# The third mixer burst of a batch moves from behind tile 0 to behind the 64-row tile 24

## The chip, the cores and the metric

One core of a Trainium2 chip runs the kernel. The metric is device time in microseconds (us), taken as the median of several runs. The engines are TensorE (PE, its weight loads PEld), VectorE (DVE), ScalarE (ACT), GpSimd (POOL) and SyncE (SP). Transfers are issued from SP (all DMA transposes, and the stores of the last batch) and from POOL (all loads, and the other stores).

## What is computed

Eight batches, each with a gated attention without softmax and, on its result, a low-rank token mixer and a channel mixer:

```python
scores = (1/S) * z @ z.T                  # S = 3136, z has 64 columns
x      = u * (max(scores, 0)**2 @ v)      # u, v, x: 3136 x 256
xm     = x + (x.T @ U @ V).T              # rank 32
out    = xm + max(xm @ w_ch1, 0) @ w_ch2  # 256 -> 1024 -> 256
```

## The kernel before

**Tiles.** The 3136 rows of a batch are 25 row tiles: 24 of 128 rows, and tile 24 (`NF`) of 64. Output tiles are worked off in the order 12, 13, ..., 24, 0, 1, ..., 11 (`turns(i) = (12 + i) % 25`), so place `i` = 12 is tile 24 and place 13 is tile 0. `FIRST` is 12 and `AHEAD` is 4.

**Scores and strips.** The squared scores are symmetric, so `A[j]` holds only 13 blocks, (j, j) to (j, j+12). `score_steps(b, j, k0, k1)` gives the steps that make blocks k0 to k1: two matmuls into one of two buffers of a PSUM pair (L307), a relu on ACT (L320), a square on DVE (L322). The other 12 blocks that output tile o needs are transposes: `turn(b, o)` issues one DMA transpose on SP (L342) of `A[o][:, 128:]` into a `strip`, one of five buffers that go round in the order of the calls. `attend_steps(b, o)` gives the 25 steps of an output tile; steps 0 to 12 read blocks of `A`, the later ones the strip of o. In steady work `turn` is called four places ahead, at the end of place `i` for the tile of place `i + 4`. Batch 0 starts before all scores are there, so it has its own tables: `first_at` says which scores are made within which place (spread evenly over its 25 steps), `first_turns` which strips are turned at the end of it:

```python
if b == 0 and i in first_turns:
    for t in first_turns[i]:
        turn(b, t)
elif i + AHEAD < NT:
    turn(b, turns(i + AHEAD))
```

**Accumulators.** An output tile accumulates in two PSUM banks, one for the upper and one for the lower 64 rows of every block (L380, matmuls that use 64 rows and 128 columns of the array, two of them side by side). Two tiles share a set of two banks: (0, 1), (2, 3), ..., (22, 23); tile 24 has a set alone. Tile 24 uses quarters of the array, 64 by 64 (L420). There are two sets, taken in turn: `open_pair` takes `sets[opened[0] % 2]` and counts `opened` up; `spare()` gives the set that no open pair holds, or, when none is open, the one that was opened last. `close_pair` adds the two banks (ACT L394, DVE L395) and multiplies by u into `x_bf` (DVE L410); for tile 24 two more copies on ACT (L406) and an addition on DVE (L407) stand between, in batch 0 four additions (L403).

**The mixer.** In places of batch b the mixer of batch b-1 runs, in 7 chunks of up to four tiles. `low_rank(b, c)` adds the low-rank part (L546, L560) and turns the chunk for the next product with a DMA transpose on SP (`turn_x`, L519, tile `ut`); chunks 4 and 5 have it within places 10 and 11. A burst n is the up-projection of chunk n (L578, full 128 by 128 array, relu on ACT L596, through the two PSUM pair buffers) merged with the down-projection of chunk n-1 (L625, added on DVE L639, through the banks of `spare()`). Bursts run in pairs at the end of four places: (0, 1) at 4, (2, 3) at 8, (4, 5) at 13, (6, 7) at 17. Burst 4 begins with the down-projection of the 64-row tile of the batch before (L625 with 64 columns of weights: the array is used as 128 by 64). With the bursts go the loads of v for the next batch and the stores of the result, on POOL's queue.

**What sets the order.** The order on each engine is the order in which the program was written out; nothing is rescheduled. PE, SP and POOL each work through one queue in that order.

Of the kernel before, what the change touches and what calls it, by code (L numbers as in the profile page):

```python
# [42 lines left out]
def kernel(  # L43
# [19 lines left out]
    NF = S // P  # L63
# [8 lines left out]
    FIRST = HALF  # L72
# [2 lines left out]
    NG = 4  # L75
    XR = 32
    XB = 28

    ctx.enter_context(
        tc.manual_schedule(engines={ENG.PE, ENG.SP, ENG.Pool, ENG.DVE, ENG.Activation})  # L80
# [17 lines left out]
    opened = [0]  # L98

    def spare():  # L100

        return sets[(opened[0] + (0 if acc else 1)) % 2]
# [29 lines left out]
    def turns(i):  # L132
        return (FIRST + i) % NT
# [19 lines left out]
    def group(b, c):  # L153
        n = len(chunks[c])
        flat = x_bf[:, ((XB // 4) * b + c) % (XR // 4), : n * D]
        return flat.rearrange("p (a t c) -> p a t c", a=ND, c=P)

    def x_at(b, t, n=1):

        c, k = offset[t]  # L160
        return group(b, c)[:, :, k : k + n, :].rearrange("p a t c -> p t a c")
# [7 lines left out]
    def load_z(b, parts):  # L169
        if b not in z_raw:  # L170
            z_raw[b] = stage.tile([P, NT, dqk], BF16, name="z_c")
        z_c = z_raw[b]
        for t0, t1 in parts:
            pool_dma(out=z_c[:, t0:t1, :], in_=rows(z[b])[:, t0:t1, :])
            if t1 == NF:
                for r in halves:
                    pool_dma(out=z_c[r, NF, :], in_=z[b, NF * P :, :])
# [4 lines left out]
    def double_z(b, parts):  # L182
        if b not in z_tiles:
            z_tiles[b] = stage.tile([P, NT, 2, dqk], BF16, name="z_bf")
        z_c, z_bf = z_raw[b], z_tiles[b]
        for t0, t1 in parts:
            for h in range(2):
                nc.vector.tensor_copy(
                    out=z_bf[:, t0 : upto(t1), h, :], in_=z_c[:, t0 : upto(t1), :]
                )  # L190

    def turn_z(b, parts):
        z_bf = z_tiles[b]
        for t0, t1 in parts:
            transpose(
                out=zT_of(b)[:, t0 : upto(t1), :],
                in_=z_bf[:, t0 : upto(t1), :, :].rearrange("p t h c -> p (t h c)"),
            )
# [37 lines left out]
    def extend_z(b):  # L236
        zT = zT_of(b)
        nc.vector.tensor_copy(out=zT[:, NT:, :], in_=zT[:, :HALF, :])

    def load_v(b, part):  # L240
        t0, t1 = part
        v_bf = v_both[b % 2]
        if t0 < NF:
            pool_dma(out=v_bf[:, t0:t1, :], in_=rows(v[b])[:, t0:t1, :])  # L244
        else:
            for r in halves:
                pool_dma(out=v_bf[r, NF, :], in_=v[b, NF * P :, :])
# [76 lines left out]
    def score_steps(b, j, k0=0, k1=NB):  # L324
        steps = []
        n = (k1 - k0) * P
        parts = _ceil_div(n, 1024)
        each = n // parts
        h = each // 2
        for i in range(parts):  # L330
            at = k0 * P + i * each

            def step(at=at):
                dst = A[j][:, at : at + each].rearrange("p (i h) -> p i h", i=2)
                score(b, [(j, j * P + at + i * h, h, dst) for i in range(2)])

            steps.append(step)
        return steps
# [151 lines left out]
    def rank_once(b, ps):  # L490

        for m in range(NT):
            g = m % G
            mm(  # L494
                out=ps[g * R : (g + 1) * R, :D],
                lhsT=U_bf[:, turns(m), :],
                rhs=x_at(b, turns(m))[:, 0],
                start=(m < G),
                stop=(m + G >= NT),
            )  # L500
        t1_sb = small.tile([P, D], BF16, name="t1_sb")
        sums = both_pool.tile([P, 512], FP32, name="both")
        nc.scalar.copy(out=sums[:, :D], in_=ps[:, :D])
        for h in range(2):
            nc.vector.tensor_tensor(
                out=t1_sb[halves[h], :],
                in0=ps[halves[h], :D],
                in1=sums[halves[1 - h], :D],
                op=ALU.add,
            )  # L510
        t1[b] = t1_sb
# [148 lines left out]
    def bursts_of(b):  # L660

        out_ = []
        for c in range(NC + 1):
            alone = c == 0 or (c == NC - 1 and b == B - 2)
            up = [lambda s=s, c=c, a=alone: up_steps(c, a)[s]() for s in range(NH // 2)]
            up = up if c < NC else []
            down = down_steps(b, c - 1) if c else []
            out_.append((up, down))
        return out_
# [10 lines left out]
    def make_stored(pair, first, n=NG):  # L680

        todo = []
        for j in pair:
            k0, k1 = first - j, min(NB, first + n - j)
            todo.append((j, first * P, (k1 - k0) * P, A[j][:, k0 * P : k1 * P]))
        score(0, todo)
# [145 lines left out]

    first_at = {8 + n: [(t, 0, NB)] for n, t in enumerate((23, 24, 0, 1, 2))}
    first_at.update({13: [], 14: []})
    for j, i in zip(range(3, FIRST), (10, 11, 12, 13, 13, 13, 14, 14, 14)):
        first_at[i].append((j, 0, FIRST - j))
    first_more = {8: (LEAD - 1, LEAD - 2), 9: (LEAD - 3, LEAD - 4)}
    first_turns = {8: (23,), 9: (24,), 10: (0,), 11: (1,), 12: (2,), 13: (3, 4)}

    next_at = {i: [] for i in range(NT)}  # L840
    for j in range(FIRST):
# [17 lines left out]
    for b in range(B):  # L859
        more = b + 1 < B  # L860
        begin = 0 if b else 2 * NG
        bursts = bursts_of(b - 1) if b else []
        burst_at = {4: (0, 1), 8: (2, 3), 13: (4, 5), 17: (6, 7)}
        own = own_at if b else first_at
        v_at = dict(zip((14, 16, 18, 20, 22, 10), V_PARTS[3:]))
        ahead = dict(zip((2, 3, 6, 7, 10, 11, 14), range(NC)))
        for i in range(begin, NT):
            o = turns(i)
            fill = [s for key in own.get(i, ()) for s in score_steps(b, *key)]
            if b == 0 and i in first_more:  # L870
                fill.append(lambda pair=first_more[i]: make_stored(pair, LEAD + 2 * NG))
            if more:
                coming = next_at if b else after_first
                fill += [s for key in coming[i] for s in score_steps(b + 1, *key)]
                if b and i == (1 if b > 1 else 5):
                    load_z(b + 1, WHOLE)
                if b == 0 and i == 9:
                    double_z(b + 1, ((FIRST, NF), (0, FIRST)))
                if i == (7 if b > 1 else 11 - 2 * b):
                    turn_z(b + 1, ((FIRST, NF),))  # L880
                if i == (10 if b else 12):
                    turn_z(b + 1, ((0, FIRST),))
                if b == 0 and i in v_at:
                    load_v(b + 1, v_at[i])
                if i == (12 if b else 14):
                    extend_z(b + 1)
            main = attend_steps(b, o)
            if b and i in ahead:
                at = 17 if (i + (i > FIRST)) % 2 == 0 else 12 if i == 7 else 10
                main.insert(at, lambda c=ahead[i]: low_rank(b - 1, c))  # L890
            _spread(main, fill)
# [5 lines that stand above are left out]
            elif more:  # L897
                turn(b + 1, turns(i + AHEAD - NT))
            elif i == NT - AHEAD:
                turn_x(b, 0)  # L900
            if b == 0 and i in puts:
                puts[i]()
            if b and i == 0:
                rank_once(b - 1, spare()[0])
            for n in burst_at.get(i, ()) if b else ():
                up, down = bursts[n]
                if not more and n >= NC - 1:
                    late += up + (down if n == NC else [])
                    up, down = [], (down if n < NC else [])

                steps = [down.pop(0)] if n == 4 else []
                steps += _merge(up, down)
                if more:
                    loads = [lambda k=k: load_v(b + 1, V_PARTS[k]) for k in ((n,) if n < NC else (n, n + 1))]
                    steps = _merge(steps, loads)
                    if n == (1 if b > 1 else 3):
                        for k, part in ((6, (FIRST, NF)), (3, (0, FIRST))):
                            steps.insert(k, lambda part=part: double_z(b + 1, (part,)))
                run(steps)
# [4 lines left out]
    b = B - 1  # L924
# [45 lines left out]
```

## Time and profile before

| | |
|---|---|
| time, median of 3 runs | 1000.54 us (1000.4 to 1003.53) |
| span of the profiled execution | 994.5 us, 6.0 us below the median |
| PE busy | 981.0 us, 13.5 us idle in all |
| ACT busy, DVE busy | 611.7 us, 553.2 us |
| 16 DMA engines | 61.6% of the span busy for SP's queue, 28.2% for POOL's |
| granted TensorE clock | 1.00 throughout |
| L342 strip transposes | 196, 5.3 us from issue to landing in the median |
| L519 ut transposes | 56, 2.4 to 6.2 us from issue to landing, 3.7 in the median |

How to read it: a timeline line gives the start, the length, engine, source line, operation, output and inputs, the part of the array or the shape, and the count of merged instructions; in square brackets stand the engine's idle time before it and what ended that. PE's matmuls overlap, so the start of the next line, not the end of the one before, tells when PE went on. SP's lines (SPq) are the time that SP spends on issuing; the transfer lands later. "DMA to landing" is counted from the start of the issue. Batch b works from about 121 us times b minus some 15 us on; batch 0 lasts to about 110 us.

### The profile page before, as it was taken

The page shows a single profiled execution, that of the slowest core. Times are in us where ns is not written, and L with a number is a line of the kernel's source. Part 1 is how long each engine was busy: PE and PEld are TensorE (multiplying, and loading weights), DVE is VectorE, ACT ScalarE, POOL GpSimd, SP SyncE. Part 2 cuts the span into 40 slices and gives each one's busy share as a digit, 9 for nine tenths or more (in the row PEclk, how much of TensorE's full clock was granted, in tenths as well). Part 3 has the DMA queues.
Part 4 walks back from the last instruction along what each step waited for, and adds up shares of the span by engine and source line. Part 5 has one row for each costly group of instructions (what it writes and reads, how often), then busy time and mean ns, then how long its engine had stood idle before and what let it go on. Part 6 is the DMA issues. An engine that isn't in the chain of part 4 may idle for free.

```text
span 994.5 us, 31023 instructions
## 1 busy us (share of the span) xinstructions
PE 981.0 (99%) x13684; PEld 774.9 (78%) x13684; DVE 553.2 (56%) x1012; ACT 611.7 (62%) x837; POOL 170.6 (17%) x316
## 2 busy tenths in 40 slices
PE   8999999999999999999999999999999999999998
PEld 5777777887878878788787887878877788787866
DVE  6878655466544664456644566445664457542352
ACT  8967764667645776466754667466674666643154
POOL 5111022111122111221112211111112120011000
PEclk9999999999999999999999999999999999999999
DMA  9999999899898998899898997989979998678543
GB/s 189 187 199 185 189 172 184 187 174 174 145 209 168 177 167 173 176 180 172 155 185 174 186 169 144 194 176 183 166 153 197 170 186 156 128 154 155 121 98 99
DMA packets 413879, 167.95 MB, mean 169 GB/s; under 512 B 389472, under 2 KB 398368, under 8 KB 413744
## 3 DMA queue, kind: packets, MB, share of 16 engines
q1 hardware_dynamic: 385424, 99.68, 61.6%
q0 software_dynamic: 28320, 66.28, 28.2%
q8 instruction: 107, 1.75, 0.7%
q14 instruction: 28, 0.23, 0.1%
HBM read 61.88 MB, written 25.69 MB: 88 GB/s over the span
## 4 chain that ended last, share of the span: by engine, by line
PE 94%; DMA 3%; ACT 1%; DVE 1%; issue 0%; DVEq 0%
PE ps L380 49%; PE ps L578 17%; PE ps L625 17%; PE ps L307 7%; DMA strip<-A 3%; PE ps L546 1%; PE ps L420 1%; ACT A L320 1%; DMA zT<-z_bf 1%; PE ps L494 1%; DVE A L322 0%; PE ps L207 0%; PE ps L477 0%; DVE both L395 0%; PE ps L223 0%
## 5 line engine op out<-in xcount | busy, mean ns | idle before, releaser
L320 ACT ACTIVATE A<-ps 128x832 bf16<-128x832 f32 (+9 forms) x481 | 359.5, 763 | 151.2 <-PE ps L307 141.7
L380 PE MATMUL ps<-v,A 64*128 64x256 bf16 x4988 | 341.2, 269 | 1.3 <-DVE A L322 1.1
L322 DVE TENSOR_TENSOR A<-A 128x832 bf16<-128x832 bf16 (+9 forms) x481 | 244.4, 524 | 130.5 <-ACT A L320 128.6
L380 PE MATMUL ps<-v,strip 64*128 64x256 bf16 x4420 | 307.7, 269 | 4.3 <-DMA strip<-A 4.2
L380 PEld LDWEIGHTS <-A 64*128 64x128 bf16 x4988 | 246.4, 94 | 45.1 <-issue 9.2
L596 ACT ACTIVATE relu_bf<-ps 128x1024 bf16<-128x1024 f32 (+2 forms) x206 | 186.3, 912 | 139.3 <-PE ps L578 139.3
L380 PEld LDWEIGHTS <-strip 64*128 64x128 bf16 x4420 | 222.8, 94 | 39.4 <-DMA strip<-A 6.1
L639 DVE TENSOR_TENSOR o_sb<-ps,x_bf 128x512 f32<-128x512 f32 (+2 forms) x105 | 69.9, 665 | 238.0 <-PE ps L625 220.1
L625 PE MATMUL ps<-w_bf,relu_bf 128*128 128x256 bf16 (+1 forms) x1600 | 201.2, 273 | 0.0
L578 PE MATMUL ps<-ut,w_bf 128*128 128x512 bf16 (+2 forms) x896 | 198.6, 353 | 0.0
L625 PEld LDWEIGHTS <-relu_bf 128*128 128x128 bf16 (+1 forms) x1600 | 153.0, 98 | 45.6 <-issue 3.6
L578 PEld LDWEIGHTS <-w_bf 128*128 128x128 bf16 x896 | 84.9, 98 | 62.1 <-issue 6.4
L364 POOL DMA_DIRECT2D u_sb<-in_u_dram x96 | 53.8, 560 | 461.8 <-DVE x_bf L410 435.5
L307 PE MATMUL ps<-zT 64*128 64x416 bf16 (+9 forms) x812 | 131.6, 312 | 0.1
L394 ACT COPY both<-ps 128x512 f32<-128x512 f32 (+1 forms) x104 | 58.8, 566 | 71.9 <-PE ps L380 65.9
L652 POOL DMA_DIRECT2D out_dram<-o_sb x84 | 45.9, 547 | 269.5 <-DVE o_sb L639 269.5
L395 DVE TENSOR_TENSOR both<-ps,both 128x512 f32<-128x512 f32 (+1 forms) x104 | 69.3, 666 | 28.8 <-ACT both L394 28.2
L410 DVE TENSOR_TENSOR x_bf<-both,u_sb 128x512 bf16<-128x512 f32 (+1 forms) x104 | 69.8, 671 | 3.6
L560 DVE TENSOR_TENSOR x_bf<-ps,x_bf 128x512 bf16<-128x512 f32 (+1 forms) x112 | 65.4, 625 | 11.3 <-PE ps L546 11.3
L307 PEld LDWEIGHTS <-zT 64*128 64x128 bf16 x812 | 43.0, 94 | 4.4 <-DMA zT<-z_bf 0.4
L244 POOL DMA_DIRECT2D v<-in_v_dram x61 | 34.3, 565 | 1.4 <-DMA z_c<-in_z_dram 1.1
L307 PE MATMUL ps<-relu_bf 64*128 64x416 bf16 (+9 forms) x117 | 23.8, 337 | 2.9 <-ACT A L320 2.2
(57 smaller groups left out, 204.9 us busy)
## 6 DMA issues: line engine op xcount, KB each, us to landing
u_sb<-in_u_dram POOLq DMA_DIRECT2D x96, 256.0 KB, 3.9
out_dram<-o_sb POOLq DMA_DIRECT2D x84, 256.0 KB, 3.1
v<-in_v_dram POOLq DMA_DIRECT2D x57, 192.0 KB, 4.5
strip<-A SPq DMA_TRANSPOSE x196, 5.3
out_dram<-o_sb SPq DMA_DIRECT2D x11, 256.0 KB, 2.0
z_c<-in_z_dram POOLq DMA_DIRECT2D x7, 384.0 KB, 5.8
u_sb<-in_u_dram POOLq DMA_DIRECT2D x16, 64.0 KB, 2.6
ut<-x_bf SPq DMA_TRANSPOSE x56, 3.7
```

What stands on the lines that cost most here:

```text
L307: mm(out=ps[:, k, :n], lhsT=zT[halves[k], j, :], rhs=zT_flat[halves[k], c : c + n], start=True, stop=True,)
L320: nc.scalar.activation(out=dst, in_=src, func=AF.Relu, scale=sc)
L322: nc.vector.tensor_tensor(out=dst, in0=dst, in1=dst, op=ALU.mult)
L380: mm(out=acc[t0][h][:, (o - t0) * D : (o - t0 + 1) * D], lhsT=w[halves[h]], rhs=v_both[b % 2][halves[h], j, :], start=start, stop=stop, **kw,)
L394: nc.scalar.copy(out=both[:, :w], in_=banks[1][:, :w])
L395: nc.vector.tensor_tensor(out=both[:, :w], in0=banks[0][:, :w], in1=both[:, :w], op=ALU.add)
L410: nc.vector.tensor_tensor(out=x_at(b, t0, n), in0=split(both[:, :w]), in1=u_sb[:, :n, :].rearrange("p t (a c) -> p t a c", c=P), op=ALU.mult,)
L560: nc.vector.tensor_tensor(out=q, in0=split(ps[h][:, : len(ks) * D]), in1=q, op=ALU.add)
L578: mm(out=ps[i][:, :w] if apart else ps[:, i, :w], lhsT=w1_bf[:, db, (hp + i) * P : (hp + i + 1) * P], rhs=uT[c][:, db, len(chunks[c]) * P ...
L596: nc.scalar.activation(out=relus[c][:, hp : hp + 2, :w], in_=ps[:, :, :w], func=AF.Relu)
L625: mm(out=ps[r, k * D : (k + 1) * D], lhsT=relus[c][:, ht, q : q + (TAIL if two else P)], rhs=w2_bf[:, ht, :], start=(ht < 1 + two), stop=( ...
L639: nc.vector.tensor_tensor(out=o_sb[:p].rearrange("p t (a c) -> p t a c", c=P), in0=split(ps[:p, k0 * D : (k + 1) * D]), in1=x_at(b, t, nk) ...
```

## The change

The third pair of bursts stands at place 12 (behind tile 24) and no longer at place 13 (behind tile 0). Tile 0 thereby moves behind the bursts. As no pair is open there, `opened` is counted up by one first: `spare()` then gives the bursts the set that tile 24 does not use, and tile 0 opens tile 24's set after them. In batch 0, which has no bursts, no scores are made within place 12 any more: the whole of tile 2 and the part of tile 5 that stood there go to place 13, and tile 8 from place 13 to place 14. `first_turns` no longer has an entry for place 12: tile 2 is turned with 3 and 4 at the end of place 13.

```diff
+    BEHIND = NF - FIRST
...
     first_at.update({13: [], 14: []})
-    for j, i in zip(range(3, FIRST), (10, 11, 12, 13, 13, 13, 14, 14, 14)):
+    first_at[13], first_at[12] = first_at[12], []
+    for j, i in zip(range(3, FIRST), (10, 11, 13, 13, 13, 14, 14, 14, 14)):
         first_at[i].append((j, 0, FIRST - j))
...
-    first_turns = {8: (23,), 9: (24,), 10: (0,), 11: (1,), 12: (2,), 13: (3, 4)}
+    first_turns = {8: (23,), 9: (24,), 10: (0,), 11: (1,), 13: (2, 3, 4)}
...
-        burst_at = {4: (0, 1), 8: (2, 3), 13: (4, 5), 17: (6, 7)}
+        burst_at = {4: (0, 1), 8: (2, 3), BEHIND: (4, 5), 17: (6, 7)}
...
+            if b and i == BEHIND:
+                opened[0] += 1
             for n in burst_at.get(i, ()) if b else ():
```

The number of instructions on PE, ACT, DVE and POOL stays the same. On SP the built program has one more: in batch 0 place 12 now falls to the `elif` above, which turns the tile of place 16, tile 3. SP's order there was zT, strip of 1, zT, strips of 2, 3, 4, 5; it is now zT, strip of 1, zT, strips of 3, 2, 3, 4, 5. The first strip of 3 is read by nothing.

## The prediction

> **What bounds the kernel now.** First the page, for the busy shares: PE works 99% of the span and idles 13.5 us in all, so no other engine matters unless it makes PE wait, and a gain can only come from PE time that does no multiplying.
>
> ```profile
> PE 981.0 (99%) x13684; PEld 774.9 (78%) x13684; DVE 553.2 (56%) x1012; ACT 611.7 (62%) x837; POOL 170.6 (17%) x316
> ```
>
> Next PE's timeline around the third bursts, here of batch 2.
>
> ```profile
> 282.76 1.36 PE L380 MATMUL ps<-v,strip 64*128 64x256 bf16 x22
> 284.05 0.85 PE L420 MATMUL ps<-v,A 64*64 64x256 bf16 x24
> 284.73 0.82 PE L420 MATMUL ps<-v,strip 64*64 64x256 bf16 x24
> 285.39 0.27 PE L420 MATMUL ps<-v,A 64*64 64x256 bf16 x1
> 285.59 0.94 PE L380 MATMUL ps<-v,A 64*128 64x256 bf16 x14
> ...
> 288.30 0.27 PE L380 MATMUL ps<-v,A 64*128 64x256 bf16 x2
> 288.51 0.63 PE L625 MATMUL ps<-w_bf,relu_bf 128*64 128x256 bf16 x8
> 289.07 1.04 PE L578 MATMUL ps<-ut,w_bf 128*128 128x512 bf16 x4
> ```
>
> Starts tell what is lost. L380 matmuls follow each other at 0.055 us (14 in 285.59 to 286.36). The 22 from 282.76 should end at 283.96 and the next kind starts at 284.05; the two from 288.30 should end at 288.41 and L625 starts at 288.51. So each change of the way the array is divided costs about 0.1 us, and there are five from tile 24 to the end of the bursts: into L420, back to L380, into L625 with 64 columns, into L578, back to L380.
>
> Third, PE's timeline of batch 0 through places 12 to 18.
>
> ```profile
> 57.13 0.41 PE L420 MATMUL ps<-v,A 64*64 64x256 bf16 x8
> 57.47 0.35 PE L307 MATMUL ps<-relu_bf 64*128 64x416 bf16 x2
> 57.75 0.63 PE L420 MATMUL ps<-v,A 64*64 64x256 bf16 x16
> ...
> 59.96 0.72 PE L380 MATMUL ps<-v,A 64*128 64x256 bf16 x10
> ...
> 67.83 1.48 PE L380 MATMUL ps<-v,strip 64*128 64x256 bf16 x24 [0.46 <-DMA strip<-A]
> ...
> 79.54 0.61 PE L380 MATMUL ps<-v,strip 64*128 64x256 bf16 x8 [2.17 <-DMA strip<-A]
> ```
>
> Here PE does wait: tile 2 for its strip until 67.83, tile 5 for its strip until 79.54. The DMA engines are the reason (shown busy in nearly every slice of 60 to 90). SP's own timeline, asked for in short windows, has the strips of 2 and 3 right behind a zT transpose; the same queries say that they land 5.7 and 6.8 us after their issue, and the strip of 5 (issued at 68.60) 10.9 us after.
>
> ```profile
> 58.77 3.17 SPq L195 DMA_TRANSPOSE zT<-z_bf  x1
> 62.04 1.45 SPq L342 DMA_TRANSPOSE strip<-A  x1
> 63.58 2.15 SPq L342 DMA_TRANSPOSE strip<-A  x1
> ```
>
> **Part 1, batch 0's scores out of tile 24.** Tile 24 with three scores inside takes 57.13 to 59.96, 2.83 us; without them in batch 2, 284.05 to 285.59, 1.54. The scores' columns are 0.54 us (416, 416 and 448, each pair side by side, at the 0.425 ns a column of L625, of which eight of 256 columns take 0.87 us in the bursts). So 2.83 - 1.54 - 0.54 = 0.75 us goes to six changes of division, and PE reaches the strip of tile 2 that much earlier, at 67.83 - 0.65 - 0.75 = 66.4 (0.65: 24 matmuls from 65.90 end at 67.2). Price: 0.75 us if nothing later in batch 0 waits. But something does.
>
> **Part 2, batch 0's strips.** Two things happen on SP. At 62.04 stands no longer the strip of 2 but the unused strip of 3, whose data are there; the strip of 2 comes second. Its data are later as well: both halves of tile 2's scores now run in place 13, and on DVE behind tile 24's closing (L395, four L403, L410: 0.42 + 1.78 + 0.42 us), so the squares end near 63.8 in place of about 61; that costs 0.2 us beside 63.58, the second slot. So the strip of 2 takes the slot that the strip of 3 had, landing near 63.58 + 6.8 = 70.4, and PE waits from 66.4 to 70.4: at this point it is 2.6 us behind the old 67.83. From there to the strip of 5 it has 77.37 - 67.83 = 9.54 us of work and comes at 79.97, after the old landing, 79.5; but that strip has one transpose more ahead of it in a full queue. What one costs there: at least its issue, 1.45 us; at most the mean distance of landings in this stretch, from 67.7 (strip of 2) to 88.1 (strip of 8, issued at 80.08, 8.0 us to land), six in 20.4, 3.4 us each; the strip of 3 landed 2.6 us behind that of 2. I take 2.0, nearer the issue, as PE's delay also moves the u and v loads that share the engines: the strip of 5 lands at 81.5, and PE is 2.0 us later than before. The old wait of 2.17 us swallows part 1 and most of the wait at tile 2. Ends: 0, if the strip of 5 is not later than PE, and 3.4. A gain is excluded, since the transposes ahead of the strip of 5 can only be more. The strips behind it move along, as PE does. Two more things hide in the same waits: place 13 now has five scores, some 4.2 us on ACT (0.82 each) in 3.4 us of PE, so PE can wait for a PSUM pair by a few tenths; and the unused strip takes one of the five buffers, so that the strip of 4 has that of tile 0, which is done some 3 us before.
>
> The Trainium skill, "DMA: Bandwidth & Descriptors", section Latency and other measured facts, gives DMA transposes 261 GB/s; by that, 128 x 1536 two-byte elements would be an estimate of 1.5 us, and batch 0 would lose 1.5 in place of 2.0. The rows above decide here, as POOL's loads run beside.
>
> **Part 3, the bursts behind tile 24.** The sequence is now L380, L420, L625, L578, L380: four changes in place of five, 7 batches x 0.1 = 0.7 us gained. I price the new change (quarters to 128 by 64), which no row shows, between 0 and 0.2 us like its neighbours, so the part is 0 to 1.4 us. In batch 1 a wait of 0.3 us for zT, now hidden behind the bursts, goes too.
>
> The Trainium skill, "TensorEngine Tiling (Array Packing)", Key Properties, says that switching the division drains TensorE, for any switch; with the 0.17 us that "TensorE: Matmul & The Clock Gate", Single matmul latency, gives as a matmul's constant part, the estimate would be 1.2 us rather than 0.7. The measured 0.1 stands.
>
> **Part 4, what the bursts now find.** They come 2.9 us earlier (285.59, not 288.51) against everything on SP, and the first up-projection stands 0.56 us behind that. It needs `ut` of chunk 4, issued shortly before tile 24:
>
> ```profile
> 160.51 1.63 SPq L519 DMA_TRANSPOSE ut<-x_bf  x1
> ...
> DMA to landing us min/median/max: 5.7/5.7/5.7
> ```
>
> In batch 1 it lands at 166.2. PE is at L578 at 164.28 + 0.56 = 164.84 and waits 1.35 us; before, it came at 168.08, with 1.9 us to spare. Batch by batch (issue + landing against the end of tile 24 + 0.76): batch 2 285.4 against 286.15, batch 4 528.2 against 528.1 (0.1 wait), 5 648.2 against 649.2, 6 769.1 against 770.2, 7 886.80 + 5.1 = 891.9 against 891.14 (0.75 wait); batch 3 not told, 402.78 + 3.7 (median) = 406.5 against 407.1. Sum 2.2 us. Chunk 5 clears: in batch 4, 532.9 against 533.3; in batch 1, 171.3 against 171.4. As landings scatter from 2.4 to 6.2 us, I allow 0.5 to 4.
>
> Behind the waiting matmul stands all of PE; it is time lost for good, since no later wait takes it up. And ACT is not free yet:
>
> ```profile
> 287.04 0.82 ACT L406 COPY both<-both 64x256 f32<-64x256 f32 x2 [1.06 <-DVE both L395]
> ...
> 290.20 1.03 ACT L596 ACTIVATE relu_bf<-ps 128x1024 bf16<-128x1024 f32 x1 [1.77 <-PE ps L578]
> ```
>
> The first relu could start 1.69 us behind the burst's start, at 287.28, but tile 24's copies hold ACT to 287.86; it ends at 288.9, and the third up-projection, which needs that PSUM buffer, is due at 288.75. About 0.2 us, in the five batches without a long `ut` wait: 1.0 us (0 to 1.5). The spare set itself is free (L394 and L395 of pair (22, 23) end by 285.5). POOL's stores and v loads come 3 us earlier and the u load of (2, 3), queued behind them, later; it is used two places on.
>
> **Sum.** 2.0 - 0.7 - 0.3 + 2.2 + 1.0 = +4.2 us on the profiled 994.5. The runs' median lies 6.0 above that span, and I add the same 4.2 there: 1004.7. The ends: 0 + 0.5 + 0 - 1.4 - 0.3 = -1.2, and 3.4 + 4 + 1.5 - 0.3 = +8.6. Both at once are unlikely; eight times in ten I expect 1000.8 to 1008.2. A measurement of this kernel tells a change from none at about 0.3%, 3.0 us.
>
> **Rivals.**
> Hidden strip: POOL's later loads give the extra transpose free room, so the strip of 5 lands before 80 and PE loses only 0.4 us in batch 0; the `ut` waits stay below 1.5. Then 0.4 - 1.0 + 1.5 + 0.5 = +1.4, 1001.9, within 0.3%. For it: the DMA view of 55 to 85 has an empty slice near 78. Against: SP issues back to back from 58.77 to 94.
> Faster: the place is the change of division at tile 24. It decides if one costs 0.6 us or more, 7 x 0.6 = 4.2, with part 2 and `ut` hidden: 1000.5 - 4.2 - 0.3 + 1.0 = 997. Against: five changes read in batch 2 all cost 0.09 to 0.13.
> Late chunks: DMA scatter makes both `ut` of every batch late by half a us: 14 x 0.5 = 7 us, and 2.0 - 1.0 + 7 + 1.0 = +9, 1009.5. Against: for chunk 4, four of seven have 0.6 us or more in hand.
> That the change does nothing is excluded by the order on PE and SP.
>
> **Chances.** Slower as summed 0.53, late chunks 0.10, hidden strip 0.33, faster 0.04. So slower 0.63, within 0.3% 0.33, faster 0.04.
>
> **What would show it.** Right: in batch 0, tile 24 takes 1.5 us, and PE waits about 4 us for the strip of 2 and 1 to 2 for that of 5; L578 waits for `ut` over 1 us in batch 1; the third up-projection step (L578) waits for ACT by 0.2 in batches 2 to 6. Wrong: strip waits in batch 0 below 3 us in all, no wait on `ut`, or changes of division far from 0.1.

## The result, and the profile after

The changed kernel takes 1003.45 us (median of 20 runs, 1000.56 to 1008.33) against 999.42 us for the kernel before, run beside it (20 runs, 995.38 to 1004.76). The ratio is 1.0042, with a 95% interval of 1.0025 to 1.0059: slower by some 4.2 us. Two runs that lie over 1.5% above the fastest of their kernel, one of run 7 below and one of the kernel before, are left out of all ratios. The profiled execution has a span of 1001.0 us against 994.5, and a mean granted clock of 0.997 against 1.00. The source lines that are named have a number one higher than before (L380 is now L381, L578 L579, and so on).

First the page's busy times of the changed kernel, then two lines of its view of waits (engine, line, releaser, us in total, how often, the longest), and last the line on strips from the same view of the kernel before.

```profile
PE 980.6 (98%) x13644; PEld 779.7 (78%) x13684; DVE 552.2 (55%) x1012; ACT 612.0 (61%) x837; POOL 170.4 (17%) x316
```
```profile
PE ps L381 <- DMA strip<-A: 5.2, 3, 4.0
PE ps L579 <- DMA ut<-x_bf: 3.1, 5, 1.1
```
```profile
PE ps L380 <- DMA strip<-A: 4.2, 5, 2.2
```

PE's busy time stays as it was (980.6 against 981.0, with 40 of its 13684 matmuls missing from this profile), so the 6.5 us are mostly idle time, and, as will be seen, busy time at half the clock. The line on `ut` is new: five waits. The strips, in total, are waited for only 1.0 us longer, but 4.0 of the 5.2 now come in one piece.

PE's timeline of the changed kernel around the third bursts of batch 2, the stretch shown of before:

```profile
287.01 1.36 PE L381 MATMUL ps<-v,strip 64*128 64x256 bf16 x22
288.31 0.85 PE L421 MATMUL ps<-v,A 64*64 64x256 bf16 x24
288.99 0.82 PE L421 MATMUL ps<-v,strip 64*64 64x256 bf16 x24
289.64 0.27 PE L421 MATMUL ps<-v,A 64*64 64x256 bf16 x1
289.84 0.63 PE L626 MATMUL ps<-w_bf,relu_bf 128*64 128x256 bf16 x8
290.76 1.04 PE L579 MATMUL ps<-ut,w_bf 128*128 128x512 bf16 x3 [0.29 <-DMA ut<-x_bf]
```

From the last quarter-array matmul to L626 it is 0.20 us, just as it was to L380 before (285.39 to 285.59): the new change of array division costs what its neighbours cost, and one change is gone. But from L626 to L579 it is now 0.92 us instead of 0.56: the wait for `ut`.

PE's timeline of batch 0 in the changed kernel, and SP's lines of the two strips that stand ahead:

```profile
56.98 0.85 PE L421 MATMUL ps<-v,A 64*64 64x256 bf16 x24
...
58.32 0.27 PE L421 MATMUL ps<-v,A 64*64 64x256 bf16 x1
59.16 0.50 PE L381 MATMUL ps<-v,A 64*128 64x256 bf16 x6 [0.58 <-DVE both L396]
...
65.62 1.49 PE L381 MATMUL ps<-v,A 64*128 64x256 bf16 x24
71.07 2.74 PE L381 MATMUL ps<-v,strip 64*128 64x256 bf16 x24 [3.96 <-DMA strip<-A]
...
76.11 0.57 PE L381 MATMUL ps<-v,A 64*128 64x256 bf16 x4
76.52 0.60 PE L381 MATMUL ps<-v,strip 64*128 64x256 bf16 x8
```
```profile
61.80 1.46 SPq L343 DMA_TRANSPOSE strip<-A  x1
...
63.52 2.10 SPq L343 DMA_TRANSPOSE strip<-A  x1
```

The second of SP's lines is the strip of 2, issued behind the unused strip of 3; it lands at 71.03, and PE waits for it almost 4 us. Then the 24 matmuls from 71.07 take 2.74 us, where they took 1.48 before: PE runs at half speed. The wait of 2.17 us for the strip of 5 is gone; that strip lands at 76.74, earlier than the 79.49 of before.

Matching the two traces matmul by matmul gives the difference by stretch. Batch 0 costs 3.5 us by 80 us into the span; the third bursts, from tile 24 to tile 1, cost 0.73, 0.27, 0.10, 0.38, 0.08, 0.71 and 0.52 in batches 1 to 7, together 2.8. Another 0.3 is lost in batch 4 ahead of its burst: at 525.04 PE waits for accumulator banks that VectorE's addition L640 frees, and this addition had waited 3.82 us for a store of the result to land. The rest stands within 0.1.

### The profile page after: what moved, and what is told of

It reads as the page before. It is cut to its first block, busy times and chain, and to the rows that moved or that the text cites. A ratio compares the mean times of both kernels' runs of the same rounds, so it can differ in the third digit from the quotient of the medians.

```text
span 1001.0 us, 30979 instructions
## 1 busy us (share of the span) xinstructions
PE 980.6 (98%) x13644; PEld 779.7 (78%) x13684; DVE 552.2 (55%) x1012; ACT 612.0 (61%) x837; POOL 170.4 (17%) x316
## 3 DMA queue, kind: packets, MB, share of 16 engines
q8 instruction: 107, 1.75, 0.7%
## 4 chain that ended last, share of the span: by engine, by line
PE 89%; DMA 6%; ACT 2%; DVE 2%; issue 1%; POOL 0%; DVEq 0%; POOLq 0%; ACTq 0%
PE ps L381 47%; PE ps L579 16%; PE ps L626 16%; PE ps L308 7%; DMA ut<-x_bf 2%; DMA strip<-A 2%; ACT A L321 2%; DMA out_dram<-o_sb 1%; PE ps L547 1%; PE ps L495 1%; DVE A L323 0%; DVE x_bf L561 0%; DVE o_sb L640 0%; PE ps L208 0%; PE ps L421 0%
## 5 line engine op out<-in xcount | busy, mean ns | idle before, releaser
L381 PE MATMUL ps<-v,A 64*128 64x256 bf16 x4988 | 341.2, 270 | 2.0 <-DVE A L323 1.1
L381 PE MATMUL ps<-v,strip 64*128 64x256 bf16 x4420 | 308.4, 270 | 5.2 <-DMA strip<-A 5.2
L381 PEld LDWEIGHTS <-A 64*128 64x128 bf16 x4988 | 248.5, 94 | 44.5 <-issue 8.5
L381 PEld LDWEIGHTS <-strip 64*128 64x128 bf16 x4420 | 224.2, 94 | 39.3 <-DMA strip<-A 6.1
L579 PE MATMUL ps<-ut,w_bf 128*128 128x512 bf16 (+2 forms) x856 | 196.6, 352 | 5.2 <-DMA ut<-x_bf 3.1
L626 PE MATMUL ps<-w_bf,relu_bf 128*128 128x256 bf16 (+1 forms) x1600 | 201.2, 273 | 0.1
L640 DVE TENSOR_TENSOR o_sb<-ps,x_bf 128x512 f32<-128x512 f32 (+2 forms) x105 | 69.8, 665 | 232.3 <-PE ps L626 198.2
L626 PEld LDWEIGHTS <-relu_bf 128*128 128x128 bf16 (+1 forms) x1600 | 153.0, 98 | 45.5 <-issue 3.5
L579 PEld LDWEIGHTS <-w_bf 128*128 128x128 bf16 x896 | 84.8, 98 | 66.0 <-issue 6.1
L396 DVE TENSOR_TENSOR both<-ps,both 128x512 f32<-128x512 f32 (+1 forms) x104 | 69.3, 667 | 28.5 <-ACT both L395 28.0
```

The costliest lines, as they stand in the source:

```text
L381: mm(out=acc[t0][h][:, (o - t0) * D : (o - t0 + 1) * D], lhsT=w[halves[h]], rhs=v_both[b % 2][halves[h], j, :], start=start, stop=stop, **kw,)
L396: nc.vector.tensor_tensor(out=both[:, :w], in0=banks[0][:, :w], in1=both[:, :w], op=ALU.add)
L579: mm(out=ps[i][:, :w] if apart else ps[:, i, :w], lhsT=w1_bf[:, db, (hp + i) * P : (hp + i + 1) * P], rhs=uT[c][:, db, len(chunks[c]) * P ...
L626: mm(out=ps[r, k * D : (k + 1) * D], lhsT=relus[c][:, ht, q : q + (TAIL if two else P)], rhs=w2_bf[:, ht, :], start=(ht < 1 + two), stop=( ...
L640: nc.vector.tensor_tensor(out=o_sb[:p].rearrange("p t (a c) -> p t a c", c=P), in0=split(ps[:p, k0 * D : (k + 1) * D]), in1=x_at(b, t, nk) ...
```

## The experiments

Each kernel was timed in five rounds beside the kernel before, 12 runs each (8 for the sixth). "Full clock" counts the runs whose mean granted clock was 0.999 or 1.0. The others show 0.998 or less, which over some 1000 us takes 3 us or more at half clock (0.0015 x 1000 / 0.5); that is, they had a drop of the clock. Of the kernel before itself, 71 of 112 runs beside the experiments had the full clock. The last columns are the profiled executions, matched matmul by matmul against the one of before: batch 0 up to 80 us, and all of batches 1 to 7.

| | ratio to before, 95% | median us | full clock | batch 0 | batches 1 to 7 |
|---|---|---|---|---|---|
| the change | 1.0042 (1.0025 to 1.0059) | 1003.45 | 0 of 20 | +3.5 | +3.1 |
| 1 no unused strip | 1.0028 (1.0004 to 1.0052) | 1001.36 | 3 of 12 | +0.2 | +2.5 |
| 2 bursts alone | 1.0002 (0.9974 to 1.0031) | 999.17 | 9 of 12 | +2.6 | +2.8 |
| 3 batch 0 alone | 1.0032 (1.0008 to 1.0055) | 1002.82 | 0 of 12 | +4.4 | +6.0, 4.7 of it with a chance drop of the clock |
| 4 work behind the wait | 1.0058 (1.0036 to 1.0080) | 1005.78 | 0 of 12 | +5.8 | +1.1 |
| 5 work in the wait | 1.0009 (0.9987 to 1.0032) | 999.50 | 11 of 12 | +1.7 | +0.8 |
| 6 ut early | 1.0069 (1.0044 to 1.0094) | 1005.02 | 3 of 8 | -0.6 | +9.4, a drop of the clock among it |
| 7 v loads later | 1.0049 (1.0015 to 1.0083) | 1004.36 | 3 of 12 | -2.1, then +4.4 by 109 us | +1.3 |
| 8 tile 2 kept | 1.0033 (0.9998 to 1.0068) | 1000.12 | 9 of 12 | -1.2 | +5.1 |
| 9 unused strip alone | 1.0041 (1.0008 to 1.0074) | 1003.18 | 2 of 12 | +1.4 | +5.7, a chance drop among it |
| 10 zT copy later | 1.0013 (0.9986 to 1.0040) | 999.39 | 10 of 12 | +0.9 | +3.3 |
| 11 zT copy later, ut early | 0.9980 (0.9953 to 1.0007) | 996.72 | 8 of 12 | +7.3, two drops among it | +0.6 |
| 12 the same again | 0.9977 (0.9950 to 1.0005) | 995.62 | 11 of 12 | -2.4 | +0.6 |

Runs 2, 6, 10, 11 and 12 have batch 0 as it was before, and yet their profiles stand anywhere from -2.4 to +7.3 there: the strips of batch 0 land at other times in every execution. One profile shows what a wait looks like; what it costs on average only the runs say.

### 1. The change without the unused strip

```diff
-    first_turns = {8: (23,), 9: (24,), 10: (0,), 11: (1,), 13: (2, 3, 4)}
+    first_turns = {8: (23,), 9: (24,), 10: (0,), 11: (1,), 12: (), 13: (2, 3, 4)}
```

> The change, but the unused strip of tile 3 is not turned (place 12 of batch 0 turns nothing). Extra-transpose theory: the strip of 2 goes out at about 63.8 as the first behind zT and lands near 69.3, 1.7 us earlier than the 71.0 of the changed kernel; PE waits about 2.5 us, the stretch at half clock is shorter or gone, and the kernel is 2 to 3.5 us faster than the change (about 1000.5 to 1001.5 where the change has 1003.5). Rival, late scores: the strip of 2 is late because tile 2's scores were moved behind tile 24, not because of the transpose ahead of it; then the strip lands at 70.5 or later and less than 0.7 us is won.

The strip of 2 was issued at 63.65, no earlier than in the change (63.52), as its data were not there, and landed at 70.37, 0.7 us earlier. So the lateness of tile 2's scores alone makes PE wait until 70.4; taking the extra transpose away mends little at that place, much as the rival had it. The ratio fell from 1.0042 to 1.0028, 1.4 us, less than the 2 to 3.5 of the theory, and with intervals that overlap.

### 2 and 3. The two halves of the change

Run 2 keeps batch 0's tables as before and moves the bursts; run 3 keeps the bursts at place 13 and takes the new tables. Run 3's edit, against the changed kernel:

```diff
-            burst_at = {4: (0, 1), 8: (2, 3), BEHIND: (4, 5), 17: (6, 7)}
+            burst_at = {4: (0, 1), 8: (2, 3), 13: (4, 5), 17: (6, 7)}
...
-            if b and i == BEHIND:
-                opened[0] += 1
```

> The third bursts behind tile 24 as in the change, batch 0's tables as before. Theory (ut and relu waits cost more than the change of division brings): +2 to +3 us against the kernel before, spread over batches 1 to 7, none in batch 0. Rival, all of the loss sits in batch 0: this version is 0.7 to 1 us faster than before.

> Batch 0's tables as in the change (with the unused strip), the bursts at place 13 as before. Theory: +3 to +4 us against before, all by 80 us: a wait of about 4 us for the strip of 2, and about 5.5 us at half clock behind it. Rival, all of the loss sits in the bursts: within 0.7 us of before.

Batch 0 alone gives 1.0032 and the bursts alone 1.0002, together 1.0034, which the interval of the change covers. So in the runs most of the loss is batch 0's. That the bursts cost 2.8 us in the profile of run 2 and 0.2 us (-2.6 to +3.1) in its runs is no contradiction within the interval, but it decides neither for the theory (+2 to +3) nor for its rival (0.7 to 1 us faster).

Run 3 has the half clock at the same place as the change (from 70.79 to 77.62, PE waiting until 71.71), in its profile, and a drop of the clock somewhere in all of its 12 runs; the change has one in 20 of 20. The later, chance drop (674.95 to 678.37) follows a wait of 2.84 us at 674.24 for VectorE's L640, which had itself waited 4.09 us for a store of the result.

### 4 and 5. PE kept at work in the wait

PE's busy time by stretches of 3.41 us, cut where the clock changes: the length, then busy us, with the number of instructions, of PE, PEld, DVE, ACT and POOL, then the granted clock (PEclk), the share of the DMA engines and GB/s. First the changed kernel, then run 1, cut on its own edges (counted on in steps of 3.413 us from the first one in its trace, at 3.97), and last PE's line of run 1's wait.

```profile
62.84:66.25 3.41, 3.41 (x70) 3.41 (x67) 3.41 (x8) 2.76 (x7) 0.99 (x2) 1.00 1.04 206
66.25:69.66 3.41, 0.86 (x16) 0.58 (x12) 3.38 (x8) 0.18 (x1) 1.03 (x2) 1.00 1.07 174
69.66:73.08 3.42, 2.01 (x20) 1.43 (x22) 0.12 (x1) 0.00 (x0) 0.25 (x1) 0.50 1.21 288
73.08:76.49 3.41, 3.41 (x38) 2.44 (x36) 0.23 (x1) 0.40 (x2) 0.00 (x0) 0.50 1.24 269
76.49:79.90 3.41, 3.41 (x64) 2.86 (x60) 1.72 (x4) 2.82 (x6) 0.00 (x0) 1.00 1.49 136
```
```profile
65.41:68.82 3.41, 1.84 (x36) 1.56 (x31) 3.38 (x9) 0.85 (x3) 0.06 (x1) 1.00 1.17 134
68.82:72.24 3.42, 1.82 (x34) 1.64 (x36) 1.10 (x2) 0.00 (x0) 1.23 (x2) 1.00 1.21 292
```
```profile
70.42 1.48 PE L381 MATMUL ps<-v,strip 64*128 64x256 bf16 x24 [3.16 <-DMA strip<-A]
```

In the changed kernel PE is busy for 0.86 us of the stretch that ends at 69.66, and from there on the clock is 0.50, for two stretches; in the stretch before and again from 76.49 on it is 1.00. Run 1 waits 3.16 us, 0.8 less than the change, but half of it falls on either side of an edge, both stretches have 1.8 us of work, and the clock stays. The price can be read off: the work from 71.07 to 76.52 in the change takes 5.45 us, the same matmuls in run 1, from 70.42 to 73.24, take 2.82: 2.6 us lost.

To test it, run 5 puts 14 matmuls whose result nobody reads ahead of the waiting step, in the change otherwise unaltered. Run 4 had them one step further down.

```diff
+            if b == 0 and i == 15:
+                def idle_work():
+                    wide = v_both[0][:, :2, :].rearrange("p t d -> p (t d)")
+                    for _ in range(14):
+                        mm(out=spare()[0], lhsT=eye, rhs=wide, start=True, stop=True)
+                main.insert(12, idle_work)
```

> The change, with 14 useless matmuls of 512 columns (about 3.0 us, into a set of banks that nothing reads) in front of the strip of 2's first use in batch 0. If PE's idling itself lowers its clock: the clock stays at 1.0 through 69 to 77, and the kernel is 2 to 2.7 us faster than the change although PE does more work. Rival, the clock falls for another reason, or the slow matmuls wait for data: the half clock stays, and the time is equal to the change's or longer.

> As e4_busy_wait, but with the 14 useless matmuls (3.0 us) one step earlier, ahead of the first use of the strip of 2, where e4 had them behind it. If PE's idling itself lowers its clock: the share of runs with a clock below 0.999 falls from all to less than half, the profile shows full clock through 69 to 77, and the kernel is 1.5 to 2.7 us faster than the change. Rival, the slow stretch has another cause (the transfers that run then): the clock falls as in the change, time equal or longer.

Run 4 missed its aim: inserted at 13, the extra work stands behind the first use of the strip, so PE waits as long as before (4.87 us before 71.21) and then does the useless work too. It tells nothing of the clock but that the drop is there. In run 5 it stands ahead (PE's timeline; of the 14 matmuls 13 are in the trace):

```profile
68.17 3.18 PE L895 MATMUL ps<-v,eye 128*128 128x512 bf16 x13 [0.55 <-DVE both L396]
71.42 1.48 PE L381 MATMUL ps<-v,strip 64*128 64x256 bf16 x24
```

The strip lands at 71.38, just as the useless work ends, so that work costs nothing, and the 24 matmuls behind it take 1.48 us again. The ratio is 1.0009 against the change's 1.0042: more work on PE and some 3 us less time, with 11 of 12 runs at full clock where the change has none of 20. Taken as independent, the two ratios differ by 0.0033 with a half width of 0.0028. The transfers are the same as in the change and run on beside the useless work (184 and 248 GB/s from 67.78 to 71.19 and on to 74.60), so the rival falls: it is PE's idling that lowers the clock, and the half clock is the larger part of batch 0's loss.

### 6. The ut transposes one place earlier

Run 2 with `low_rank` of chunks 4 and 5 within places 9 and 10 rather than 10 and 11.

```diff
-        ahead = dict(zip((2, 3, 6, 7, 10, 11, 14), range(NC)))
+        ahead = dict(zip((2, 3, 6, 7, 9, 10, 14), range(NC)))
```

> As e2_bursts_only, with the low-rank part and the ut transposes of chunks 4 and 5 one place earlier (places 9 and 10). Theory: no wait of L578 for ut in the third bursts any more, the wait for ACT's relu (0.2 us a batch) stays; batches 1 to 7 gain 1.5 to 3 us against e2's profile, so 0.997 to 1.000 of the kernel before. Rival, the transposes only move the jam on SP, and strips are late in their place: no gain against e2.

A miss, and a useful one. The first L579 no longer waits (165.54, 0.56 us behind L626), but the second round of it does. VectorE's lines of batch 1, then PE's:

```profile
167.04 0.56 DVE L239 COPY zT<-zT 128x1536 bf16<-128x1536 bf16 x1 [1.45 <-DMA zT<-z_bf]
167.52 0.42 DVE L396 TENSOR_TENSOR both<-ps,both 128x256 f32<-128x256 f32 x1
```
```profile
169.88 1.02 PE L579 MATMUL ps<-ut,w_bf 128*128 128x512 bf16 x4 [1.57 <-ACT relu_bf L597]
```

The copy into zT (L239) stands ahead of tile 24's closing in VectorE's order, and waits for a z transpose. The closing, ScalarE's two copies and the first relu wait behind it, and PE for the relu: +1.4 us in batch 1, +1.7 in batch 3, +1.4 in batch 4. In batch 6 the same wait is 2.04 us long (PE goes on at 781.22), the clock is at a half from 781.32 to 784.73, and +3.8 is lost.

### 7 and 8. Other ways to ease batch 0

Run 7 is the kernel before with the v loads of batch 1 later (places 18, 19, 20, 22, 23 instead of 14, 16, 18, 20, 22); run 8 is the change with tile 2's scores and its turn left in place 12 and only the parts of tiles 5 and 8 moved.

> The kernel before, with batch 0's loads of the next batch's v at places 18, 19, 20, 22, 23 in place of 14, 16, 18, 20, 22. If the DMA engines' load is what makes the strips of batch 0 late: the strips of 2 and 5 land 1 to 3 us earlier, fewer runs than one in three have a clock below 0.999, and the time is 1 to 2 us below before. Rival, the transposes alone fill the engines: strips as late as before, within 0.5 us.

> The change, but tile 2's scores stay within tile 24 and its strip is turned at the end of place 12 as before; the others are moved as in the change. If the lateness of tile 2's scores and strip is what costs batch 0 its time (extra transpose and late scores together): batch 0 as in the kernel before or 0.25 us better (two of the six changes of division saved), a clock below 0.999 in less than half of the runs, and 2.5 to 4 us faster than the change. Rival, moving tiles 5 and 8 with their five scores in place 13 jams ACT and costs by itself: still 1 us or more slower than e2_bursts_only.

In run 7 the strip of 5 landed at 75.25, earlier than in any of the six profiles with the same tables and the loads where they were (77.1 to 84.5), and its wait was gone; so the loads probably share in its lateness. The strip of 2 came no earlier (68.05). But another strip was late 24 us on (a wait of 1.75 us at 103.78), the clock fell to a half at 105.29, 9 of 12 runs had a drop, and the time rose to 1.0049: the forecast for the time failed. In run 8 the strip of 2 landed at 68.47, batch 0 was 1.2 us ahead of before, and 9 of 12 runs kept the full clock, as expected. Its median lies 0.4 us above that of before beside it (1000.12 and 999.76); its ratio of 1.0033 has an interval that reaches below 1, and one run of 1013.33 us weighs in it. In its profile batches 1 to 7 stand at +5.1. Of that, 2.3 us are lost in batch 5, where PE waits for VectorE's addition L640 and this for a store of the result. VectorE's line, then PE's:

```profile
643.53 0.69 DVE L640 TENSOR_TENSOR o_sb<-ps,x_bf 128x512 f32<-128x512 f32 x1 [6.54 <-DMA out_dram<-o_sb]
```
```profile
644.27 1.60 PE L381 MATMUL ps<-v,A 64*128 64x256 bf16 x26 [2.10 <-DVE o_sb L640]
```

### 9. The unused strip alone

The kernel before with `12: (3, 2)` in `first_turns` and nothing else.

> The kernel before with one edit: the unused transpose of tile 3 stands ahead of the strip of 2 in batch 0; scores and bursts stay where they were. Theory of the prediction (part 2): the strip of 2 lands one slot later, at about 70.4 us instead of 67.8, and the strip of 5 has 2.0 us more ahead of it, so batch 0 loses 1.5 to 3.4 us. Rival, from the run without the unused strip, where the strip of 2 landed only 0.7 us earlier than in the change: the extra transpose costs 0.7 us or less, batch 0 stays within +0.7 of before by 80 us, and the time within 0.1% of before, unless the clock drops.

PE's timeline:

```profile
69.88 1.48 PE L380 MATMUL ps<-v,strip 64*128 64x256 bf16 x24 [2.36 <-DMA strip<-A]
...
74.38 0.61 PE L380 MATMUL ps<-v,strip 64*128 64x256 bf16 x8 [1.51 <-DMA strip<-A]
```

The strip of 2 lands at 69.83, 2.0 us later than before, where 2.6 was expected and the rival had 0.7 or less. One execution can't settle this: with SP's order of before that strip landed between 67.4 and 69.7 in the seven other profiles. But the strip of 5, at 79.92, was only 0.4 us later than before (79.49), and by then PE, held up at the strips of 2 and 3, had no need to wait for it; the price of 2.0 us for one transpose more is not seen there, and batch 0 lost 1.4 us. Late data alone (run 1) make the strip of 2 land 2.6 us later, the extra transpose alone 2.0, both (the change) 3.2: in these profiles each is most of the delay by itself, which fits that removing one of them brings little. In the runs the edit does cost: 10 of 12 had a drop of the clock (11 of 29 of the kernel before beside it), and the ratio is 1.0041. The profile's own drop, in batch 5, follows a wait of 2.46 us at 645.59 for VectorE's L639 and so for a store, as in runs 3 and 8.

### 10, 11 and 12. A version with the waits taken out

VectorE's, ScalarE's and PE's lines of the quiet batch 3 in the changed kernel:

```profile
411.62 0.55 DVE L239 COPY zT<-zT 128x1536 bf16<-128x1536 bf16 x1
412.09 0.42 DVE L396 TENSOR_TENSOR both<-ps,both 128x256 f32<-128x256 f32 x1
...
412.55 0.82 ACT L407 COPY both<-both 64x256 f32<-64x256 f32 x2 [1.06 <-DVE both L396]
413.39 3.22 ACT L597 ACTIVATE relu_bf<-ps 128x1024 bf16<-128x1024 f32 x3
...
413.40 2.08 PE L579 MATMUL ps<-ut,w_bf 128*128 128x512 bf16 x8
```

The step from 413.40 is, in the kernel before:

```profile
411.80 1.89 PE L578 MATMUL ps<-ut,w_bf 128*128 128x512 bf16 x8
```

In the changed kernel, without a wait for a transfer, the zT copy still pushes the closing back by 0.5 us, ScalarE's first relu starts at 413.39, and the second and third up-projection together take 2.08 us instead of 1.89. Run 10 is run 2 with that copy one place later; runs 11 and 12 are run 10 with `ut` early as in run 6.

```diff
-                if i == (12 if b else 14):
+                if i == (13 if b else 14):
                     extend_z(b + 1)
```

> Bursts behind tile 24 with batch 0's tables as before, and in batches 1 to 7 the copy into zT (VectorE, L239) one place later, behind the bursts instead of ahead of tile 24's closing. Theory: the closing of tile 24 no longer waits on VectorE behind that copy, the copies of tile 24 on ScalarE end earlier and the 0.2 us wait of the third up-projection for the relu goes: quiet batches (3, 5) come out at -0.1 us against before where bursts alone gave +0.09; waits for ut stay (batch 1 about 1 us, others 0 to 0.7). Rival: the relu wait is set by the copies on ScalarE themselves and stays: quiet batches +0.09 as before.

> As the run with the later zT copy, and the ut transposes of chunks 4 and 5 issued one place earlier (within places 9 and 10 instead of 10 and 11). Theory: with the zT copy out of the way of the closing neither ut nor relu is waited for, so every third burst is at -0.1 us against before (the saved change of division), some -0.7 us over the seven, and the time 0.1% below before (0.998 to 1.000 of it) at an equal clock. Rival: something else that stood ahead of the bursts (the z transpose in SP's queue, landing at 167.0 in batch 1) is waited for in turn, and batches 1, 3 and 4 lose over 0.5 us each, as in the run with ut early alone (+1.4 to +1.7).

> The kernel of the run before (zT copy later, ut early, batch 0 as in the kernel before) once more, since its interval of 0.9953 to 1.0007 touches 1. Theory: the seven third bursts save 0.1 us each and batch 1's zT wait of 0.3 is gone, about -1 us, and the time is 0.997 to 1.000 of before. Rival: the first result came from a lucky share of runs without a clock drop, and this one lies at 1.000 to 1.003. Third bursts are expected at -0.1 us in most batches in either case.

Run 10: the moved bursts of batches 2, 3, 5 and 6, which met no wait, stand at -0.10 to -0.11 against before, where run 2 had +0.09 in all four. The 0.2 us of relu wait came from the copy. The wait for `ut` stays (1.4 us in batch 1), and other bursts and places had waits of their own.

The same lines of batch 3 in run 12:

```profile
404.41 0.42 DVE L396 TENSOR_TENSOR both<-ps,both 128x256 f32<-128x256 f32 x1
...
404.86 0.82 ACT L407 COPY both<-both 64x256 f32<-64x256 f32 x2 [0.58 <-DVE both L396]
405.70 1.02 ACT L597 ACTIVATE relu_bf<-ps 128x1024 bf16<-128x1024 f32 x1
...
406.19 1.89 PE L579 MATMUL ps<-ut,w_bf 128*128 128x512 bf16 x8
```

The up-projection is back at 1.89 us. In runs 11 and 12 alike the moved burst, from tile 24 to tile 1, stands at -0.42 in batch 1 and at -0.10 to -0.11 in batches 2 to 7, as expected; no wait for `ut` is left in it, and no z transpose is waited for. But 0.07 a batch is lost again at places 9 to 11, where the low-rank part now runs a place earlier, so that most batches end at -0.03 to -0.04. Batch 5 lost 0.8 and 1.2, outside the moved burst, at L579 (for `ut`, near 633 and 623) and at L547 (near 648 and 638), where PE again waits for VectorE's L640 and this for a store (3.18 and 3.53 us). The runs stand at 0.9980 and 0.9977 of before, each with an interval that just reaches past 1. Taken as independent, their mean is 0.9979 with a half width of 0.0027 divided by the root of 2, 0.0019: faster than before by a narrow margin, and clearly faster than the change (1.0042). How much of the 2 us is the edit's doing is open. The moved bursts give 1.1 us by the profiles, 0.5 of it lost again at places 9 to 11; and of these runs 19 of 24 had the full clock, of the kernel before beside them 28 of 46. Whether that is the edit or chance isn't shown.

## Why the prediction was right, and where not

**The sum was right, its terms in part.** +4.2 us was predicted on the median, and 4.2 us (0.0042 of 999.4) came out; the time itself lies 1.3 us below the 1004.7 mainly because the kernel before took 999.42 beside it and not 1000.54. In the profile the loss is 6.5, rounded: 3.5 for batch 0 (predicted 2.0), 2.8 for the bursts (predicted 2.2) and 0.3 for the wait for a store. The profile of the kernel before is one without a drop of the clock, which its runs often have; the prediction added its terms to a median 6.0 us above that profile's span without asking what stands in the 6.0 (in the changed kernel span and time differ by 1.8: 1001.0 and 1002.79). In the runs batch 0 weighs more still (1.0032 against 1.0002).

**Part 1, right in the main.** Tile 24 takes 1.5 us in batch 0 (56.98 to about 58.5), as said, and the gain was swallowed by the strip's wait. Not foreseen: place 13 (tile 0) can't open until VectorE has added the banks (L396, 0.58 us at 59.16), so some 0.6 of the 0.75 would have been lost even without the strip.

**Part 2, right at the strip of 2, wrong behind it.** It was to land at 70.4 with PE waiting for 4 us; it landed at 71.03 with a wait of 3.96. The step that failed is "the strip of 5 lands at 81.5, and PE is 2.0 us later than before": it landed at 76.74, 6 us ahead of PE's need at 83.06, and between 77.4 and 79.3 in runs 1, 3, 4 and 5, which have the same tables or nearly so. With the tables of before it landed anywhere from 77.1 to 84.5 (runs 2, 6, 10, 11 and 12): the 79.49 was one draw from a wide scatter, not a fixed date to add a slot to. What goes with the earlier landing is that PE's delay holds back POOL's next u and v loads too, which were issued at 75.4 and 76.0 before and at 81.3 and 81.8 in the change, and that the DMA engines moved 262 GB/s while this strip was on its way (71.96 to 76.74), against 167 before (68.60 to 79.49). That the loads are the whole cause is not shown. Without the half clock batch 0 would have lost 3.5 - 2.6 = 0.9 us, not 2.0.

**The missing term.** The prediction forecast a wait of 4 us on PE and priced it as 4 us. It costs 2.6 us more, since the clock drops behind it. The Trainium skill has the rule, in "TensorE: Matmul & The Clock Gate", section What's actually happening: the clock falls to half after an idle window of about 3.4 us, in windows that run freely; this case's stretches of 3.41 us agree. The same page, Why this matters for your kernels, warns of idle gaps over about 3 us; run 1 shows that one of 3.2 us can pass, run 9 that one of 2.5 us can bring the drop, and the changed kernel that a window needn't be wholly idle (0.86 us of 3.41 were busy). Batch 0's two errors, 2.6 left out and 1.1 too much behind the strip of 5, cancel in part; that the total fits so well is in this respect luck.

**Part 3, right.** Four changes at 0.1 us: with the waits taken away the moved bursts show it in batches 2 to 7 (-0.10 to -0.11 in runs 11 and 12), and batch 1 shows the zT wait gone as well (-0.42, 0.3 more).

**Part 4, right, with the batches shifted.** The `ut` waits came to 3.4 us (the start of L579 behind L626 less 0.56: 1.16, 0.36, 0.48, 0.81 and 0.63 in batches 1, 2, 4, 6 and 7) where 2.2 was summed and 0.5 to 4 allowed. With 0.11 gained in each batch, 0.3 for zT and 0.2 for the relu in batches 3 and 5 they make up the 2.8. Batches 2 and 6 were held to have 0.8 and 1.1 us in hand and had not, since landings scatter by more than that. The relu wait is 0.2 us, as said, but only in the two batches without a `ut` wait. Its cause was half named: ScalarE's copies do stand in the way, but they are late because VectorE's zT copy stands ahead of the closing, as run 10 shows.

**The rivals.** "Hidden strip" asked that the strip of 5 cost nothing, which came true, and gave +1.4; it fell because the clock dropped and the `ut` waits passed its 1.5 us. "Faster" by dear changes of division fell: 0.1 us each. "Late chunks" fell: at most one `ut` a batch was waited for.

## What to carry to other kernels

A wait that the forecast puts at some 2 us or more on TensorE (1.75 was the shortest that brought a drop here) is to be priced twice: for itself, and, as a chance, for the work behind it at half clock. When a step is moved, look at what stands ahead of it in every engine's order, not only in the queue it waits on: the version that came out ahead has a copy on VectorE and a transpose on SP moved along with the bursts. And when the landings of a transfer scatter by some us from one execution to the next, slack of half a us in one profile is no slack.

## What the runs showed of the hardware

- The granted clock changes on a grid of 3.41 us (edges at 66.25, 69.66, 73.08 and so on in the changed kernel), and a drop lasts one or two stretches, 3.4 or 6.8 us: two where PE was busy for only 0.59 (the change) or 0.73 (run 3) of the first slow stretch, one where it was for 0.90 or more. By the profiles, up to the last matmuls, each stretch at full clock in which PE was busy for less than 40% was followed by half clock (seven of seven: 0.00, 0.04, 0.15, 0.21, 0.25, 0.28 and 0.32 of the stretch); at 0.40 to 0.49 it went either way (0.40 and 0.49 dropped, 0.44, 0.45 and 0.47 did not), and none above that dropped.
- The length of a wait alone doesn't decide: 3.16 us, spread over two stretches of that grid, left the clock as it was (run 1), while waits of 2.84 (run 3, 674.24), 2.46 (run 9, 645.59), 2.04 (run 6, 781.22) and 1.75 us (run 7, 103.78) brought a drop.
- VectorE's addition L640 (L639 before) waits for a store of the result to land, up to 6.9 us (run 9), and PE for the accumulator banks that it frees. Such waits of PE, 0.3 to 2.84 us, stand in the profiles of runs 3, 5 and 7 to 12, with the bursts at either place; in runs 3 and 9 they brought the chance drops.
- Even the kernel before has a drop in 41 of 112 runs, and those are 4.3 to 6.5 us longer in the median (997.15 and 1001.43, 996.57 and 1002.18, 995.99 and 1000.67, 996.12 and 1002.58). The half clock itself takes at most 1.7 us of that for each stretch of 3.41; the rest would be the waits that go with it, which these runs don't show apart.
